# Last two attentions: one group of float32 products for each pair of heads

## The chip, the cores and the metric

The kernel runs on one core of one Trainium2 chip. The metric is the device time of an execution in microseconds; of the kernel before, three runs gave a median of 1101.09 us (1098.07 to 1101.76). One further execution was profiled; all rows of the trace below are from it.

## The reference

Three stages follow one another: attention over four batch entries (called blocks here) with twelve heads, an MLP with squared ReLU, and a router with eight experts of limited capacity. Cut to what is computed:

```python
# q, k, v: [4, 12, 448, 64]
scores = scale * np.matmul(q, k.transpose(0, 1, 3, 2))
scores = cap * np.tanh(scores / cap)
attn = np.exp(scores - np.max(scores, axis=-1, keepdims=True))
attn = attn / (np.sum(attn, axis=-1, keepdims=True) + 1e-09)
x = np.matmul(attn, v)                  # as rows: [1792, 768]
h = x @ w_in                            # 768 -> 2048
r = np.maximum(h, 0.0)
x = (r * r) @ w_out                     # 2048 -> 768
logits = x @ w_gate                     # 768 -> 8
# greedy: the largest logits first, one expert for each token, 224 tokens for each expert
out[mask_e] = np.maximum(x[mask_e] @ w1[e], 0.0) @ w2[e]   # 768 -> 1024 -> 768
```

## The kernel before, in words

**Streams.** `run` works block by block. attention(0) runs alone, hidden(0) beside attention(1), then, for b = 2 and 3, output(b-2) and hidden(b-1) beside attention(b). `merge` interleaves such generators: each yields an amount of TensorE time, and the one that is least far on relative to its total goes next (118.0 for output and hidden together, 44.0 for an attention). For b = 2 and 3 this fixes TensorE's order as written (`manual_schedule` for PE); on the other engines a scheduler orders the instructions. Each engine works through its own queue in order.

**Attention.** A block has six pairs of heads (`hp`). `scores(hp, c)` makes the scores of the pair for a block of keys: for c = 0 to 2 two float32 products with 64 rows, one for each head (L233), for c = 3 one product with 128 rows for the last 64 keys of both heads (L235). They go to a PSUM tile `big`, of which there are two buffers. ScalarE reads it with tanh (L237), which frees the buffer, and makes the exponential in place (L238); sums `z` over the keys are made by VectorE in block 0 and by GpSimd (POOL) in the other blocks (L244, L246, L250). `pv` multiplies with v, in 64 columns for each head (L258) and in full for the last keys (L261), into a PSUM tile `aux`. `norm` sums z over the partitions with two products with ones (L266), also into `aux`; ScalarE adds eps and frees that tile (L268), VectorE takes the reciprocal (L269) and multiplies (L271). `aux` has two buffers as well. `whole = b > 1` marks the blocks 2 and 3; there a pair's float32 products stand on TensorE in three groups, with products of the MLP between: scores 0 and 1 of pair hp; pv and norm of pair hp-1; scores 2 and 3 of pair hp.

**MLP.** Its products, the main products in what follows, are float32r, in three parts (high by high, low by high, high by low): L395 to L397 in `hidden`, 18 for each of 16 weight tiles, and L452 to L454 in `output`, 12 for each of 24 tiles of w_out. `finish` (L430) transposes a finished piece of 128 columns into `aux`, ScalarE copies it (L432) and stores it. Weights arrive as 64-bit integers; for the first block VectorE decodes each tile in three operations (L328 to L330; two buffers `raw`, three `wf`), and stores it to a DRAM cache, from which the later blocks load it. Each tile is split: ScalarE casts the high part `wh` (L356), VectorE or POOL subtracts the low part `wl` (L357), three buffers each. So in the first part of block 2, where output(0) runs beside attention(2), the tiles of w_out are decoded while the attention's tanh and exp share ScalarE's queue with the casts. `split_rows` casts the attention's result into x high and low (L316 for the low part).

Of the kernel before, what the change touches and what calls it, by code (L numbers as in the profile page):

```python
# [23 lines left out]
HP = NH // 2  # L24
# [55 lines left out]
class Kernel:  # L80
# [125 lines left out]
    def attention(self, b):  # L206

        nc, ap = self.nc, self.ap
        qk, P, vt, zs, U = {}, {}, {}, {}, {}
        adder = nc.vector if b == 0 else nc.gpsimd  # L210

        def load(hp):
            qk[hp] = t = ap.tile([128, QK], F32, name="qk", bufs=3)
            if b + hp == 0:
                for half, q in ((0, nc.sync), (1, nc.scalar)):
                    q.dma_start(t[half * 64:half * 64 + 64], self.q_k[b, hp, half * 64:half * 64 + 64])
            else:
                nc.sync.dma_start(t, self.q_k[b, hp])

        def load_v(hp):  # L220
            vt[hp] = ap.tile([128, KB + 1, 2 * DH], F32, name="v", bufs=3)
            nc.sync.dma_start(vt[hp], self.v[b, hp])

        def scores(hp, c):

            t = qk[hp]
            n = 2 if c < KB else 1
            k, q = t[:, c * 128:(c + 1) * 128], t[:, QK - S:]
            ps = self.psum.tile([128, 2, 512], F32, name="big")
            if c < KB:  # L230
                for s in range(2):
                    rows = slice(s * 64, s * 64 + 64)
                    nc.tensor.matmul(ps[:, s, :S], k[rows], q[rows], start=True, stop=True)  # L233
            else:
                nc.tensor.matmul(ps[:, 0, :S], k, q, start=True, stop=True)  # L235
            p = ap.tile([128, n, S], F32, name=f"p{n}", bufs=(2, 5)[n - 1])
            nc.scalar.activation(p, ps[:, :n, :S], AF.Tanh, scale=self.isc)  # L237
            e = nc.scalar.activation(p, p, AF.Exp, scale=self.capt)  # L238
            if b == 0:
                self.exps.append(e)  # L240
            P[hp, c] = p
            if c == 1:
                zs[hp] = z = ap.tile([128, 2, S], F32, name="z", bufs=2)
                adder.tensor_add(z, P[hp, 0], p)  # L244
            elif c == 2:
                adder.tensor_add(zs[hp], zs[hp], p)  # L246
            elif c == KB:
                for s in range(2):
                    half = slice(s * 64, s * 64 + 64)
                    adder.tensor_add(zs[hp][half, s], zs[hp][half, s], p[half, 0])  # L250

        def pv(hp, c0, c1):
            if c0 == 0:
                U[hp] = self.psum.tile([128, S], F32, name="aux")
            for c in range(c0, c1):
                if c < KB:
                    for s in range(2):
                        nc.tensor.matmul(U[hp][s * 64:s * 64 + 64], vt[hp][:, c, s * 64:s * 64 + 64], P[hp, c][:, s],  # L258
                                         start=(c == 0), stop=False, skip_group_check=True)
                else:  # L260
                    nc.tensor.matmul(U[hp], vt[hp][:, c], P[hp, c][:, 0], start=False, stop=True, skip_group_check=True)  # L261

        def norm(hp):
            z = self.psum.tile([128, S], F32, name="aux")
            for s in range(2):
                nc.tensor.matmul(z[s * 64:s * 64 + 64], self.ones, zs[hp][:, s], start=True, stop=True)  # L266
            d = ap.tile([128, S], F32, name="d", bufs=1)
            (nc.vector.tensor_scalar(d, z, self.eps, None, op0=OP.add) if b == 0 else nc.scalar.activation(d, z, AF.Identity, bias=self.eps))  # L268
            nc.vector.reciprocal(d, d)  # L269
            x = self.xq.tile([128, S], F32, name="x")  # L270
            m = nc.vector.tensor_mul(x, U.pop(hp), d)  # L271
            if b == 0:
                self.norms.append(m)
            if b == NB - 1:
                self.mark = m
            self.x_t[b, hp] = x

        load(0)
        load(1)
        load_v(0)  # L280
        whole = b > 1
        for hp in range(HP + 1):
            if hp < HP:
                if hp + 2 < HP:
                    load(hp + 2)
                if hp + 1 < HP:
                    load_v(hp + 1)
                scores(hp, 0)
                if not whole:
                    yield 0.8  # L290
                scores(hp, 1)
                yield 1.6 if whole else 0.8
            if hp:
                pv(hp - 1, 0, 2)
                if not whole:
                    yield 1.6
                pv(hp - 1, 2, 4)
                if not whole or hp == HP:
                    yield 1.6
                norm(hp - 1)  # L300
                yield 4.0 if whole else 0.8
            if hp < HP:
                scores(hp, 2)
                if not whole:
                    yield 0.8
                scores(hp, 3)
                yield 1.4 if whole else 0.6

    def split_rows(self, b):
        nc = self.nc  # L310
# [641 lines left out]
```

## Time and profile before

| what | value |
|---|---|
| median of three runs | 1101.09 us (1098.07 to 1101.76) |
| the profiled execution, its own time | 1098.67 us |
| its span, first to last instruction | 1096.8 us |
| mean granted clock of TensorE | 0.990 |
| busy: TensorE (PE) | 97% |
| busy: VectorE (DVE) | 62% |
| busy: ScalarE (ACT) | 50% |
| busy: GpSimd (POOL) | 32% |

The profiled execution lies 2.4 us under the median. Shares are of the span. Matmuls are pipelined and their ends are modelled, so how long one takes is read from start to start. In the trace's rows an operation names the tile that it writes, an arrow and the tiles that it reads, then the shapes; in square brackets stands how long its engine was idle before it and what ended that. The blocks whose order changes, 2 and 3, run from 187 to 343 and from 359 to 515 us.

### The profile page before, as it was taken

Reading aid. Unit: us, or ns where it says so; the run is one execution under the profiler, and the core shown is the slowest. Engines: PE = TensorE matmul, PEld = TensorE weight load, DVE = VectorE, ACT = ScalarE, POOL = GpSimd, SP = SyncE. Lnnn points to the kernel's source line nnn. Section 1 sums busy time; section 2 is a strip of 40 time slices with the busy share of each in tenths; the row PEclk is TensorE's granted clock in tenths of the full one; section 3 lists DMA queues with packets and bytes.
Section 4 is the critical chain, followed back from the end, with each engine's and each line's share of the span. In section 5 each row is a group of like instructions: output and inputs, shape, how many; then the busy total and the mean of one; then the engine's idle time right before and its main releaser. Section 6 shows DMA issues by size and latency. Waiting matters only on the chain.

```text
span 1096.8 us, 15959 instructions
## 1 busy us (share of the span) xinstructions
PE 1063.3 (97%) x5866; PEld 836.7 (76%) x5866; DVE 676.2 (62%) x1124; ACT 543.8 (50%) x843; POOL 351.0 (32%) x245
## 2 busy tenths in 40 slices
PE   6999999999999999999999999999899999999997
PEld 2336655776677677677787888888799899999996
DVE  5987999978545478788411355565666554555551
ACT  5876776444776744676654222222222223554551
POOL 0127776655221322221443444444210201220000
PEclk9999999999999999999999999999899999999999
DMA  7533655566533377765563233336472465965530
GB/s 278 195 117 124 218 187 203 184 237 232 158 100 95 95 226 245 251 223 200 183 213 95 67 95 103 94 104 213 153 279 70 153 215 179 307 216 185 200 111 26
DMA packets 79454, 187.20 MB, mean 171 GB/s; under 512 B 8528, under 2 KB 19312, under 8 KB 79376
## 3 DMA queue, kind: packets, MB, share of 16 engines
q1 hardware_dynamic: 64736, 169.24, 46.0%
q0 software_dynamic: 3424, 11.19, 3.4%
q10 hardware_dynamic: 11216, 5.75, 2.0%
q8 instruction: 46, 0.75, 0.3%
q14 instruction: 32, 0.26, 0.1%
HBM read 156.26 MB, written 29.88 MB: 170 GB/s over the span
## 4 chain that ended last, share of the span: by engine, by line
PE 65%; issue 12%; DVE 10%; DMA 8%; ACT 2%; POOL 1%; SPq 1%; POOLq 0%; DVEq 0%; ACTq 0%
PE big L877 6%; PE acc L395 6%; PE acc L452 6%; PE acc L396 6%; PE acc L397 6%; PE acc L454 5%; PE acc L453 5%; PE acc L839 5%; PE aux L258 3%; PE big L233 3%; DMA raw<-w_out 3%; PE aux L653 2%; DVE wf L329 2%; DVE wf L328 2%; PE acc L846 2%
## 5 line engine op out<-in xcount | busy, mean ns | idle before, releaser
L356 ACT CAST wh<-wf 128x512 fp32r<-128x512 f32 (+1 forms) x187 | 135.2, 723 | 268.5 <-PE acc L453 102.2
L357 POOL TENSOR_TENSOR wl<-wf,wh 128x512 fp32r<-128x512 f32 (+1 forms) x97 | 156.5, 1616 | 206.5 <-ACT wh L356 196.9
L395 PE MATMUL acc<-xh,wh 128*128 128x448 f32 x384 | 148.6, 389 | 2.0 <-ACT r L402 2.0
L452 PE MATMUL acc<-g,wh 128*128 128x448 f32 x384 | 150.4, 392 | 0.0
L396 PE MATMUL acc<-xl,wh 128*128 128x448 f32 x384 | 141.2, 368 | 1.9 <-DVE xl L316 1.9
L454 PE MATMUL acc<-g,wl 128*128 128x448 f32 x384 | 140.4, 366 | 1.2 <-DVE wl L357 1.2
L397 PE MATMUL acc<-xh,wl 128*128 128x448 f32 x384 | 140.4, 366 | 0.1
L453 PE MATMUL acc<-g,wh 128*128 128x448 f32 x384 | 139.9, 364 | 0.0
L357 DVE TENSOR_TENSOR wl<-wf,wh 128x768 fp32r<-128x768 f32 (+1 forms) x90 | 88.0, 979 | 61.1 <-ACT wh L356 60.3
L877 PE MATMUL big<-wh,g 128*112 128x384 f32 x512 | 117.8, 342 | 0.0
L237 ACT ACTIVATE p<-big,isc 128x896 f32<-128x896 f32 x96 | 85.7, 907 | 26.9 <-PE big L233 26.7
L395 PEld LDWEIGHTS acc<-xh,wh 128*128 128x128 f32 x384 | 72.1, 189 | 35.1 <-issue 15.7
L238 ACT ACTIVATE p<-p,capt 128x896 f32<-128x896 f32 x96 | 89.4, 949 | 1.3
L756 POOL DMA_INDIRECT xg<-x,idx x32 | 34.2, 1068 | 169.9 <-PE acc L775 93.3
L877 PEld LDWEIGHTS big<-wh,g 128*112 128x112 f32 x512 | 86.8, 175 | 0.8
L407 DVE TENSOR_TENSOR g<-r,g 128x448 fp32r<-128x448 f32 x58 | 49.4, 851 | 60.2 <-ACT g L406 57.6
L246 POOL TENSOR_TENSOR z<-z,p 128x896 f32<-128x896 f32 x18 | 38.9, 2162 | 146.4 <-ACT p L238 144.1
L452 PEld LDWEIGHTS acc<-g,wh 128*128 128x128 f32 x384 | 72.4, 189 | 14.4 <-issue 9.6
L396 PEld LDWEIGHTS acc<-xl,wh 128*128 128x128 f32 x384 | 72.6, 189 | 12.4 <-issue 4.1
L269 DVE RECIPROCAL d<-d 128x448 f32<-128x448 f32 x24 | 70.7, 2948 | 16.6 <-ACT d L268 16.5
L233 PE MATMUL big<-qk 64*128 64x448 f32 x288 | 74.1, 598 | 6.9 <-DMA qk<-qk 6.2
L454 PEld LDWEIGHTS acc<-g,wl 128*128 128x128 f32 x384 | 72.0, 187 | 9.4 <-DVE wl L357 2.7
(182 smaller groups left out, 1941.7 us busy)
## 6 DMA issues: line engine op xcount, KB each, us to landing
g<-w SPq DMA_DIRECT2D x68, 384.0 KB
wf<-wi SPq DMA_DIRECT2D x48, 384.0 KB
wf<-wo SPq DMA_DIRECT2D x72, 256.0 KB
wf<-w SPq DMA_DIRECT2D x36, 384.0 KB
raw<-w_in SPq DMA_DIRECT2D x16, 768.0 KB
raw<-w_out SPq DMA_DIRECT2D x24, 512.0 KB
raw<-w_out_t SPq DMA_DIRECT2D x24, 512.0 KB
wt<-wt SPq DMA_DIRECT2D x48, 256.0 KB
```

Source lines behind the costliest of these rows:

```text
L233: nc.tensor.matmul(ps[:, s, :S], k[rows], q[rows], start=True, stop=True)
L237: nc.scalar.activation(p, ps[:, :n, :S], AF.Tanh, scale=self.isc)
L238: e = nc.scalar.activation(p, p, AF.Exp, scale=self.capt)
L356: nc.scalar.copy(wh[:, :w], wf[:, :w])
L357: low.tensor_sub(wl[:, :w], wf[:, :w], wh[:, :w].bitcast(F32))
L395: nc.tensor.matmul(ps, wh[:, d], xh, start=(d == 0), stop=False)
L396: nc.tensor.matmul(ps, wh[:, d], xl, start=False, stop=False)
L397: nc.tensor.matmul(ps, wl[:, d], xh, start=False, stop=(d == ND - 1))
L452: nc.tensor.matmul(ps, a, gh, start=(f == 0), stop=False)
L453: nc.tensor.matmul(ps, a, gl, start=False, stop=False)
L454: nc.tensor.matmul(ps, z, gh, start=False, stop=(f == NF - 1))
L877: nc.tensor.matmul(acc[h][:, s, :DM // 2], l, r[:, s * (DM // 2):(s + 1) * (DM // 2)], start=(j == 0 and first), stop=(j == NF2 - 1 and last))
```

## The change

Only `attention` is edited, and only for `whole`, blocks 2 and 3. From the second pair on, the three groups become one: scores 0 and 1, the first half of pv of the pair before, scores 2, the second half of pv, scores 3, norm, and then a yield of 7.0. The first pair, which has no pair before it, makes its four blocks of scores in a row and yields 3.0. After the last pair pv and norm stand alone as before, with other yields. The amounts add up to about the same for a block, and the interleaving with the MLP changes through them.

```diff
                 scores(hp, 1)
-                yield 1.6 if whole else 0.8
+                if not whole:
+                    yield 0.8
             if hp:
                 pv(hp - 1, 0, 2)
                 if not whole:
                     yield 1.6
+                elif hp < HP:
+                    scores(hp, 2)
                 pv(hp - 1, 2, 4)
                 if not whole or hp == HP:
                     yield 1.6
+                elif hp < HP:
+                    scores(hp, 3)
                 norm(hp - 1)
-                yield 4.0 if whole else 0.8
-            if hp < HP:
+                yield 7.0 if whole else 0.8
+            if hp < HP and not (whole and hp):
                 scores(hp, 2)
                 if not whole:
                     yield 0.8
                 scores(hp, 3)
-                yield 1.4 if whole else 0.6
+                yield 3.0 if whole else 0.6
```

Lines from 306 on are numbered five higher in the changed kernel (L356 becomes L361, L430 becomes L435). On TensorE, at the products with v of pair 2 in block 2 (p_... are the tiles of exponentials, aux the PSUM tile, L452 to L454 main products), the kernel before has a group of its own for them:

```order
L454 MATMUL acc<-g,wl 128x448
L258 MATMUL aux<-p_1724,v 64x448 x2
L258 MATMUL aux<-p_1730,v 64x448 x2
L258 MATMUL aux<-p_1912,v 64x448 x2
L261 MATMUL aux<-p_1918,v 128x448
L266 MATMUL aux<-z,ones 64x448 x2
L452 MATMUL acc<-g,wh 128x448
```

and the changed kernel has:

```order
L459 MATMUL acc<-g,wl 128x448
L233 MATMUL big<-qk 128x448 x4
L258 MATMUL aux<-p_1724,v 64x448 x2
L258 MATMUL aux<-p_1730,v 64x448 x2
L233 MATMUL big<-qk 128x448 x2
L258 MATMUL aux<-p_1743,v 64x448 x2
L261 MATMUL aux<-p_1752,v 128x448
L235 MATMUL big<-qk 128x448
L266 MATMUL aux<-z,ones 64x448 x2
L435 MATMUL aux<-cf,xt 112x128 x4
L457 MATMUL acc<-g,wh 128x448
```

The scores of pair 3 (L233, L235) now stand around the products with v of pair 2, and a `finish` (L435) follows the group.

On ScalarE, the tanh and exp of the same pair 3 (p_1960 is its first block of scores), the kernel before has:

```order
L356 CAST wh<-wf 128x512 x2
L237 ACTIVATE p_1960<-big,isc 128x896
L238 ACTIVATE p_1960<-p_1960,capt 128x896
L237 ACTIVATE p_1966<-big,isc 128x896
L432 COPY rows<-aux 112x512
L238 ACTIVATE p_1966<-p_1966,capt 128x896
```

and the changed kernel:

```order
L361 CAST wh<-wf 128x512 x3
L237 ACTIVATE p_1960<-big,isc 128x896
L238 ACTIVATE p_1960<-p_1960,capt 128x896
L237 ACTIVATE p_1966<-big,isc 128x896
L238 ACTIVATE p_1966<-p_1966,capt 128x896
L237 ACTIVATE p_1979<-big,isc 128x896
L238 ACTIVATE p_1979<-p_1979,capt 128x896
L237 ACTIVATE p_1988<-big,isc 128x448
L238 ACTIVATE p_1988<-p_1988,capt 128x448
L268 ACTIVATE d<-aux,eps 128x448
L437 COPY rows<-aux 112x512
```

Now all eight operations of the pair stand together; ahead of the first tanh stands the cast of w_out tile 20 in both programs.

On VectorE, the reciprocal of pair 1 in block 2 (L269), the kernel before has it among the decodes of w_out tiles (L328 to L330), two tiles later than the changed one:

```order
L357 TENSOR_TENSOR wl<-wf,wh 128x512
L330 SCALAR_TENSOR_TENSOR wf<-raw,wf 128x512
L328 TENSOR_SCALAR wf<-raw 128x512
L329 SCALAR_TENSOR_TENSOR wf<-raw,wf 128x512
L330 SCALAR_TENSOR_TENSOR wf<-raw,wf 128x512
L269 RECIPROCAL d<-d 128x448
L328 TENSOR_SCALAR wf<-raw 128x512
L271 TENSOR_TENSOR x<-aux,d 128x448
```

and the changed kernel:

```order
L335 SCALAR_TENSOR_TENSOR wf<-raw,wf 128x512
L269 RECIPROCAL d<-d 128x448
L362 TENSOR_TENSOR wl<-wf,wh 128x512
L271 TENSOR_TENSOR x<-aux,d 128x448
L333 TENSOR_SCALAR wf<-raw 128x512 x2
L334 SCALAR_TENSOR_TENSOR wf<-raw,wf 128x512 x2
L335 SCALAR_TENSOR_TENSOR wf<-raw,wf 128x512 x2
```

The reciprocal has moved ahead of the decodes of tiles 16 and 17.

## Rows read from the trace of the kernel before

**Rows 1.** The page: busy us, share of the span, instructions of each engine.

```profile
PE 1063.3 (97%) x5866; PEld 836.7 (76%) x5866; DVE 676.2 (62%) x1124; ACT 543.8 (50%) x843; POOL 351.0 (32%) x245
```

**Rows 2.** Windows: length, busy PE, PEld, DVE, ACT, POOL; granted clock, DMA share, GB/s.

```profile
187.00:276.00 89.00, 87.19 (x407) 62.68 (x406) 74.19 (x70) 42.64 (x62) 50.29 (x31) 1.00 0.64 221
```

**Rows 3.** TensorE's waits from 187 to 515: us in total, times, longest.

```profile
PE acc L454 <- DVE wl L357: 1.2, 4, 0.5
PE aux L266 <- ACT rows L432: 1.0, 1, 1.0
```

**Rows 4.** Timeline of TensorE: start, us, instruction (modelled ends); around mode changes.

```profile
25.21 1.72 PE L258 MATMUL aux<-p,v 128*64 128x448 f32 x8
26.86 1.40 PE L233 MATMUL big<-qk 64*128 64x448 f32 x6
...
180.47 0.91 PE L261 MATMUL aux<-p,v 128*128 128x448 f32 x2
180.87 0.71 PE L453 MATMUL acc<-g,wh 128*128 128x448 f32 x1
181.42 0.36 PE L454 MATMUL acc<-g,wl 128*128 128x448 f32 x1
181.62 0.36 PE L452 MATMUL acc<-g,wh 128*128 128x448 f32 x1
...
406.42 1.02 PE L261 MATMUL aux<-p,v 128*128 128x448 f32 x2
407.37 0.97 PE L266 MATMUL aux<-z,ones 128*64 128x448 f32 x4
...
419.58 1.02 PE L235 MATMUL big<-qk 128*128 128x448 f32 x2
420.08 0.72 PE L452 MATMUL acc<-g,wh 128*128 128x448 f32 x1
420.64 0.36 PE L453 MATMUL acc<-g,wh 128*128 128x448 f32 x1
```

**Rows 5.** The same: scores 0 and 1 of two pairs.

```profile
250.71 1.77 PE L233 MATMUL big<-qk 64*128 64x448 f32 x8
...
359.58 1.77 PE L233 MATMUL big<-qk 64*128 64x448 f32 x8
```

**Rows 6.** Timeline of ScalarE: tanh behind these scores.

```profile
256.98 0.62 ACT L356 CAST wh<-wf 128x512 fp32r<-128x512 f32 x1 [4.76 <-DVE wf L330]
257.50 1.00 ACT L237 ACTIVATE p<-big,isc 128x896 f32<-128x896 f32 x1
...
360.74 0.99 ACT L237 ACTIVATE p<-big,isc 128x896 f32<-128x896 f32 x1
...
363.03 1.00 ACT L237 ACTIVATE p<-big,isc 128x896 f32<-128x896 f32 x1
```

**Rows 7.** Timeline of VectorE: decodes of w_out tiles, the last of them tile 20.

```profile
237.50 0.43 DVE L328 TENSOR_SCALAR wf<-raw 128x512 int32<-128x512 int32 x1 [2.61 <-POOL wl L357]
...
252.01 1.60 DVE L328 TENSOR_SCALAR wf<-raw 128x512 int32<-128x512 int32 x1 [0.81 <-DMA raw<-w_out]
253.64 1.67 DVE L329 SCALAR_TENSOR_TENSOR wf<-raw,wf 128x512 int32<-128x512 int32 x1
255.34 1.52 DVE L330 SCALAR_TENSOR_TENSOR wf<-raw,wf 128x512 int32<-128x512 int32 x1
```

**Rows 8.** Windows around an idle stretch of TensorE, columns as in rows 2.

```profile
100.35:102.40 2.05, 0.01 (x1) 0.01 (x1) 2.05 (x2) 0.57 (x2) 0.87 (x1) 1.00 0.00 0
102.57:105.98 3.41, 3.41 (x10) 3.03 (x11) 2.41 (x5) 3.35 (x7) 0.00 (x0) 0.50 0.78 252
```

**Rows 9.** Timeline of ScalarE: the addition of eps that frees a PSUM tile aux.

```profile
381.83 0.64 ACT L268 ACTIVATE d<-aux,eps 128x448 f32<-128x448 f32 x1 [4.72 <-PE aux L266]
```

**Rows 10.** The page's groups: busy us, mean ns of one, idle before and its releaser.

```profile
L269 DVE RECIPROCAL d<-d 128x448 f32<-128x448 f32 x24 | 70.7, 2948 | 16.6 <-ACT d L268 16.5
```

**Rows 11.** Timeline of TensorE: the start of the last hidden layer, behind block 3.

```profile
534.52 0.47 PE L396 MATMUL acc<-xl,wh 128*128 128x448 f32 x1 [1.12 <-DVE xl L316]
```

## What the change does to the time, predicted from the rows

> **What bounds the kernel now.** The page's busy line comes first: TensorE is busy for 97% of the span [rows 1], so a change pays only where it shortens TensorE's own queue or a wait in it. The change touches the attention of blocks 2 and 3 (time 187 to 343 and 359 to 515), and the windows say what stands close behind TensorE there: in block 2's first part, while w_out is still decoded, VectorE is busy for 74.19 of 89 us [rows 2]. The waits that TensorE shows in all of this come to 2.2 us: four times on VectorE's wl (1.2), once on ACT (1.0) [rows 3]. So at most some 2 us of waiting can be won; the rest has to come out of the float32 products themselves.
>
> **Mode changes.** I read starts, since ends are modelled. An L261 (all 128 rows and columns) that stands among the main products, which have the same shape, takes 180.47 to 180.87, and the first main product behind it steps 0.55 instead of 0.20: 0.40 + 0.35 = 0.75 us. Between the 64-column L258 and L266 the same L261 takes 406.42 to 407.37, 0.95; with a change on one side only (L233 ahead of L235, main products behind) it is 0.50 + 0.36 = 0.86 [rows 4]. So a change between 64 rows, 64 columns and the full array costs 0.10 us, and a change of number format alone nothing. Before, a pair has L233 L235 | L233 | L258 L261 L266 with main products between: 2 + 2 + 4 = 8 changes. After it has L233 L258 L233 L258 L261 L235 L266 in one run: 7. That is 0.10 us for each of ten pairs; each block's first pair goes from 4 changes to 2. Sum: -1.0 - 0.4 = **-1.4 us**. L258 directly beside L233 is in the trace (25.21 to 26.86, 1.65 for four products, no extra price [rows 4]). The Trainium skill's TensorEngine Tiling (Key Properties) says that a change of tiling mode drains the array; that speaks against what the change promises, since fewer groups are not fewer modes. If only a group's two ends cost, three groups into one would save 4 changes, 4.4 us in all; the rows bear out the count of modes.
>
> **The first pair's four score blocks in a row.** Scores have two PSUM buffers, so the third block waits for the first block's tanh and the fourth for the second's. In block 3 the first L233 stands at 359.58 and takes 1.7; the third block would start at 361.3, and tanh ends at 361.73: 0.5. The fourth would follow at 362.6; the second tanh (after a cast and an exp) ends at 364.03: 1.4 [rows 5, 6]. 1.9 us in block 3. In block 2 nothing shows it; between 0 and 1.9 I take 0.5, since ACT has no Relu and Square of the hidden layer pending there. Sum **+2.4**.
>
> **The later pairs: is tanh in time?** In the new group the third score block stands behind two score blocks (1.7 [rows 5]) and four products with v (1.65 [rows 4]), so 3.35 us after the group's start; it needs the first tanh done. When ACT is free this holds: the first block is done at 0.95, tanh takes 1.0. The fourth block comes 2.8 us later still and is safe. But ACT works in its queue's order, and ahead of the tanh of pair 3 in block 2 stands the cast of w_out tile 20, in both programs. In the trace that cast stood idle for 4.76 us until VectorE's decode (L330) ended, started at 256.98, and tanh at 257.50, although the scores, started at 250.71, were there from 251.7 [rows 5, 6]. Before, that cost nothing: TensorE came back to this PSUM buffer only 66 main products and all products with v later. After, it is 3.35 us away.
>
> When does the new group of pair 3 start? By the order it stands behind w_out tile 17, and by then TensorE has done exactly what it had done at 250.71 before: the scores of pairs 0 to 2 and v of pairs 0 and 1. So it starts at 250.71 - 0.4 (mode changes) + 0.5 (first pair), less up to 0.8 of the old waits: about 250.2. The third block is due at 253.6. Decode of tile 20 ended at 256.86 before [rows 7]. It may end earlier: its three operations took 1.60, 1.67 and 1.52 beside POOL's sums, while the first takes 0.43 where POOL is idle, so 1.0 us and more can go from each [rows 7], and the sums of that pair now come after its exps; 3.0 us earlier, 253.9, is the early end. It may end later: the reciprocal of pair 1 (2.95 us, as in every pair [rows 10]) now stands ahead of the decode of tiles 16 and 17, and each raw load waits for the decode two tiles before (tile 20's stood idle for 0.81 on its DMA [rows 7]): 259.8 is the late end. Cast 0.5, tanh 1.0 and 0.1 for the semaphores follow: the third block starts at 255.5 to 261.4, a wait of 1.9 to 7.8. I take the decode where the trace has it, a little earlier for the idle POOL: **+5.0 us**. Nothing else is lost behind it, since the weights catch up meanwhile.
>
> **Clock.** After an idle stretch of 2.05 us the trace has the granted clock at 0.50 (1.2 GHz) from 102.57 to 105.98, with ten main products at 0.37 instead of 0.20 [rows 8]: 1.6 us lost. A wait of 5 us should do the same: **+1.5**, between 0 and 1.6. The Trainium skill's TensorE: Matmul & The Clock Gate (Part 1) has the idle array throttled by default and released by activity; by that rule too a wait need not end in a drop each time, and without it the sum is 1.5 lower.
>
> **A transpose right behind the group.** In both blocks L430 now follows the last L266 at once (after pair 3's group). Its PSUM bank is the one that L268 frees; before, six or more main products lay between. L268 starts after L266 and takes 0.64 [rows 9]: at least 0.75 us each. ACT's eight operations of a group (about 1.0 each, half for the last two) end at 8.0 us when on time, as late as the group's products (7.8); behind the late group it is up to 1.7. Sum **+2.2** (1.5 to 3.4).
>
> **The old waits.** The four on wl came where ACT had tanh and exp ahead of a cast while TensorE used up weights; in one group TensorE uses none meanwhile, and after a long wait all tiles are ready. The one on ACT's copy (L266, 1.0) goes since the last transpose now lies at least six products and the group's own 7 us ahead. **-2.2**, with some 0.1 us for each restart -2.5; at least 0.
>
> **Other queues.** SP's loads of qk and v stand behind events that come no later than before (a pair's qk is free at its group's end): 0. POOL's sums of a pair now come in one row, ahead of its wl of tile 6 or 13; TensorE needs tile 6 only 30 main products (6.1 us) behind the group: 0. VectorE's wl of tile 14 stands behind pair 1's reciprocal: 0 to 1.5, kept for the range. After 515 the order is the same in both programs, and TensorE is the bound, so what is gained or lost is carried to the end.
>
> **Sum.** -1.4 + 2.4 + 5.0 + 1.5 + 2.2 - 2.5 = +7.2 us on the profiled execution's 1098.67 (span 1096.8 and 1.9 around it): 1105.9. The median of the runs shown, 1101.09, is 2.4 above that execution, the lowest 0.6 below; I state 1106, on the level of that execution.
>
> **Rivals.** (A) Tile 20 is decoded in time, or pair 3's group comes late enough (point: decode before 252): no wait, no drop. For it: VectorE has 15 us free in 89. Against it: ACT waited there in the trace. -1.4 + 2.4 + 1.5 - 2.5 = 0: 1099, on the median's level 1101; no change. (B) Faster: besides (A), ACT and VectorE drain during the 8 us groups, so that tanh starts within 0.1 us of the scores in the first pairs too (their waits gone) and VectorE's xl behind block 3, which TensorE waits 1.12 us for [rows 11], is in time: -1.4 - 2.5 - 1.1 + 1.5 = -3.5: 1095.2. Against it: Relu, Square and casts stand ahead of tanh in ACT's queue in block 3's first pair too. (C) Slower still: the queue of casts holds tanh in pair 2 as well (the last cast ahead of it is tile 12's, due about when the group starts) or in block 3, where the same queue waits for weights by DMA: another 3 to 5 us, 1110. (D) The change does not do what it says, a group is not cheaper: that is the mode count, and it is in the sum.
>
> **How the numbers follow.** Forecast (pair 3 waits, 1103 to 1109): 0.52. (A) 0.28. (C) 0.12. (B) 0.08. A measurement of this kernel tells about 0.3% (3.3 us) from no change, so faster 0.08, same 0.28, slower 0.64. The range for 8 in 10 takes in the forecast, most of (A) and the lower part of (C): 1098 to 1112.
>
> **What would show it.** In the changed profile: one wait of several us on TensorE between L258 and the third L233 of pair 3 in block 2, ended by ACT's tanh (L237), whose own wait was on VectorE's decode; a granted clock of 0.5 right behind; waits of 0.5 and 1.4 in block 3's first pair; L430 waiting for L268 twice; wl no longer a releaser; the end of each block shifted by +6 and then +1. If pair 3 shows no wait, the forecast is wrong and (A) holds; if TensorE's groups take over 8.3 us without waits, the price of modes is wrong.

## The result, and the profile after

The changed kernel takes 1113.71 us (median of 7 runs, 1106.73 to 1115.52) against 1101.76 us (median of 7): the ratio is 1.0101, with a 95% interval from 1.0077 to 1.0125. It is slower, as forecast, but by 12 us instead of some 5 to 7, and 1.7 us above the range.

The page's busy line (as [rows 1]; us, share of the span, instructions), and TensorE's waits from 187 to 545 us of the changed kernel (as [rows 3]; lines from 306 on are numbered five higher, L435 is the transpose):

```profile
PE 1069.1 (96%) x5866; PEld 843.8 (76%) x5866; DVE 657.6 (59%) x1124; ACT 548.2 (49%) x843; POOL 347.9 (31%) x245
```

```profile
PE big L233 <- ACT p L237: 8.3, 3, 5.4
PE aux L435 <- ACT d L268: 2.1, 2, 1.0
PE big L235 <- ACT p L237: 1.6, 2, 1.3
```

The waits for wl and for ScalarE's copy [rows 3] are gone; 12.0 us of new ones are there. The longest is the one that was forecast. These are the groups of pairs 2 and 3 of block 2 and the first pair of block 3, in TensorE's timeline:

```profile
222.37 1.77 PE L233 MATMUL big<-qk 64*128 64x448 f32 x8
224.08 1.72 PE L258 MATMUL aux<-p,v 128*64 128x448 f32 x8
228.33 1.02 PE L233 MATMUL big<-qk 64*128 64x448 f32 x4 [2.53 <-ACT p L237]
...
253.28 1.77 PE L233 MATMUL big<-qk 64*128 64x448 f32 x8
254.98 1.73 PE L258 MATMUL aux<-p,v 128*64 128x448 f32 x8
262.09 1.86 PE L233 MATMUL big<-qk 64*128 64x448 f32 x4 [5.38 <-ACT p L237]
...
370.25 1.02 PE L233 MATMUL big<-qk 64*128 64x448 f32 x4 [0.43 <-ACT p L237]
372.54 1.38 PE L235 MATMUL big<-qk 128*128 128x448 f32 x2 [1.27 <-ACT p L237]
```

On ScalarE the cast of tile 20 (L361) waits for the decode, and tanh stands behind it, as in [rows 6]; on VectorE that decode waits for its load in turn:

```profile
260.51 0.62 ACT L361 CAST wh<-wf 128x512 fp32r<-128x512 f32 x1 [2.73 <-DVE wf L335]
261.03 1.00 ACT L237 ACTIVATE p<-big,isc 128x896 f32<-128x896 f32 x1
```

```profile
257.57 0.43 DVE L333 TENSOR_SCALAR wf<-raw 128x512 int32<-128x512 int32 x1 [0.53 <-DMA raw<-w_out]
258.04 1.63 DVE L334 SCALAR_TENSOR_TENSOR wf<-raw,wf 128x512 int32<-128x512 int32 x1
259.70 0.69 DVE L335 SCALAR_TENSOR_TENSOR wf<-raw,wf 128x512 int32<-128x512 int32 x1
```

In or right behind each of these three waits the granted clock falls to 0.50. Windows, columns as in [rows 2]; the first answers to that row, the last lies far behind the change, in the experts:

```profile
187.00:276.00 89.00, 79.71 (x353) 54.85 (x353) 74.71 (x68) 44.43 (x62) 51.61 (x32) 0.94 0.60 203
229.70:233.12 3.42, 3.42 (x8) 1.18 (x4) 2.38 (x3) 3.36 (x4) 1.73 (x1) 0.50 0.70 243
260.42:267.25 6.83, 5.16 (x11) 1.66 (x12) 4.79 (x6) 6.44 (x7) 2.08 (x1) 0.50 0.70 232
373.06:376.47 3.41, 3.41 (x10) 2.69 (x9) 0.00 (x0) 3.36 (x6) 2.03 (x1) 0.50 0.39 144
874.82:885.06 10.24, 10.24 (x56) 8.90 (x55) 3.97 (x12) 0.00 (x0) 0.31 (x1) 0.50 0.06 19
```

Half of TensorE's busy time at 0.50 is lost: 1.7 and 2.6 us in block 2, 1.7 in block 3. By the starts of the same products in both traces, the changed kernel is 8.5 us behind at the end of block 2 (its first product of the next block starts at 366.7 instead of 358.3), 10.6 at the start of the last hidden layer, and 10.9 at the last product with w_out (777.6 instead of 766.7). The profiled execution (1115.52) loses another 5.9 in the experts, mostly in the stretch at 874.82. Twelve of the 16 profiled executions of this document have such a stretch, of 6.8 or 10.2 us, that starts between 858 and 875; the kernel before with a third buffer has it, the profiled execution of the kernel before does not. So it is no mark of the change. The medians lie 12.0 apart, near the 10.9 of the last product with w_out; below, the place of the last product with w_out (its shift against the kernel before) stands beside the medians.

### The profile page after: what moved, and what is told of

Same layout as the page of the kernel before. It is cut to its first block, busy times and chain, and to the rows that moved or that the text cites. A ratio compares the mean times of both kernels' runs of the same rounds, so it can differ in the third digit from the quotient of the medians.

```text
span 1113.6 us, 15956 instructions
## 1 busy us (share of the span) xinstructions
PE 1069.1 (96%) x5866; PEld 843.8 (76%) x5866; DVE 657.6 (59%) x1124; ACT 548.2 (49%) x843; POOL 347.9 (31%) x245
## 3 DMA queue, kind: packets, MB, share of 16 engines
q10 hardware_dynamic: 11216, 5.75, 1.9%
## 4 chain that ended last, share of the span: by engine, by line
PE 69%; issue 12%; DVE 7%; DMA 5%; ACT 4%; POOL 2%; SPq 0%; POOLq 0%; ACTq 0%; DVEq 0%
PE acc L400 7%; PE acc L457 6%; PE big L882 6%; PE acc L401 6%; PE acc L402 6%; PE acc L459 6%; PE acc L458 6%; PE acc L844 5%; PE aux L258 4%; PE big L233 4%; PE aux L658 2%; PE aux L261 2%; DVE wf L334 2%; PE acc L851 2%; PE aux L266 1%
## 5 line engine op out<-in xcount | busy, mean ns | idle before, releaser
L361 ACT CAST wh<-wf 128x512 fp32r<-128x512 f32 (+1 forms) x187 | 135.4, 724 | 308.2 <-PE acc L458 121.6
L400 PE MATMUL acc<-xh,wh 128*128 128x448 f32 x384 | 146.0, 382 | 2.0 <-ACT r L407 2.0
L362 DVE TENSOR_TENSOR wl<-wf,wh 128x768 fp32r<-128x768 f32 (+1 forms) x90 | 80.4, 896 | 68.5 <-ACT wh L361 67.5
L882 PE MATMUL big<-wh,g 128*112 128x384 f32 x512 | 120.3, 348 | 0.0
L244 POOL TENSOR_TENSOR z<-p,p 128x896 f32<-128x896 f32 x18 | 39.1, 2174 | 202.3 <-issue 152.6
L269 DVE RECIPROCAL d<-d 128x448 f32<-128x448 f32 x24 | 70.8, 2949 | 40.8 <-ACT d L268 40.7
L233 PE MATMUL big<-qk 64*128 64x448 f32 x288 | 75.1, 606 | 15.3 <-ACT p L237 9.1
L402 PEld LDWEIGHTS acc<-xh,wl 128*128 128x128 f32 x384 | 72.5, 189 | 6.4 <-issue 0.8
```

The source lines that it names most:

```text
L361: nc.scalar.copy(wh[:, :w], wf[:, :w])
L362: low.tensor_sub(wl[:, :w], wf[:, :w], wh[:, :w].bitcast(F32))
L400: nc.tensor.matmul(ps, wh[:, d], xh, start=(d == 0), stop=False)
L402: nc.tensor.matmul(ps, wl[:, d], xh, start=False, stop=(d == ND - 1))
L882: nc.tensor.matmul(acc[h][:, s, :DM // 2], l, r[:, s * (DM // 2):(s + 1) * (DM // 2)], start=(j == 0 and first), stop=(j == NF2 - 1 and last))
```

## The experiments

Ratios are against the kernel before, with their 95% intervals; shifts are of the last product with w_out, in the traces. When block 2 starts, ahead of every edit to the attention, the traces already lie between 1.0 us ahead of that of the kernel before and 0.3 us behind it, so a difference of less than 1 us between two shifts says nothing.

**Block 3 alone, block 2 alone.** The new grouping for one block only (`one = b == 3`, then `one = b == 2`, against the changed kernel):

```diff
-                if not whole:
-                    yield 0.8
+                if not one:
+                    yield 1.6 if whole else 0.8
...
-                elif hp < HP:
+                elif one and hp < HP:
...
-                yield 7.0 if whole else 0.8
-            if hp < HP and not (whole and hp):
+                yield (7.0 if one else 4.0) if whole else 0.8
+            if hp < HP and not (one and hp):
...
-                yield 3.0 if whole else 0.6
+                yield (3.0 if one else 1.4) if whole else 0.6
```

> Only block 3 has the one group per pair; block 2 keeps the three groups of before. Theory (TensorE waits for tanh, and tanh waits behind casts of w_out that wait for decode): no decode in block 3, so only the first pair's waits (0.4 and 1.3 us), one transpose wait (1.0) and a clock drop (1.7), less what the fewer changes of tiling save: about +2 us at the end of block 3, median 1102 to 1104. Rival (the long float32 run itself is what costs, about evenly in both blocks): +5 us, 1106 to 1108.

> Only block 2 has the one group per pair. Theory: the waits of 2.5 and 5.4 us for tanh in pairs 2 and 3 and their clock drops are all here: +8.5 us at the end of block 2 as in the changed kernel, median 1108 to 1112. Rival (cost is even over both blocks): +5 us, 1106 to 1108.

Block 3 alone: 1101.82, ratio 0.9987 (0.9965 to 1.0008), shift +1.4. Block 2 alone: 1111.52, ratio 1.0075 (1.0047 to 1.0103), shift +8.3. The cost is block 2's, where w_out is decoded; in block 3 the long groups cost nothing that a measurement can tell.

**Casts off ScalarE.** Five casts that stand ahead of the late tanh go to VectorE:

```diff
-        nc.scalar.copy(wh[:, :w], wf[:, :w])
+        early = self.ready - self.at[0, "o"] in (11, 12, 18, 19, 20)
+        (nc.vector.tensor_copy if early else nc.scalar.copy)(wh[:, :w], wf[:, :w])
```

> The changed kernel, with five casts of w_out (tiles 11, 12, 18, 19, 20) made by VectorE right behind the decode instead of by ScalarE, so that no cast that is late stands ahead of the tanh of pairs 2 and 3 in block 2. Theory: the waits of 2.5 and 5.4 us and the two drops behind them (1.7 and 2.4) go, block 2 ends 3 us or more earlier than in the kernel before rather than 8.5 later, median 1101 to 1104. Rival (decode itself is too slow for the bunched demand, and the wait only moves): TensorE then waits as long for wh or wl of tiles 13 or 21, and the median stays at 1110 or above.

1110.21, ratio 1.0088 (1.0061 to 1.0115), shift +9.6. Here the theory that I had fell. Its waits:

```profile
PE acc L460 <- DVE wl L363: 2.6, 1, 2.6
PE acc L458 <- ACT wh L362: 2.2, 1, 2.2
PE aux L436 <- ACT d L268: 2.1, 2, 1.0
PE big L235 <- ACT p L237: 1.6, 2, 1.3
PE acc L460 <- POOL wl L363: 1.2, 3, 0.6
...
PE big L233 <- ACT p L237: 0.6, 2, 0.4
```

Of the 7.9 us for tanh in pairs 2 and 3 nothing is left, and 6.0 us for wl and wh have come up on the main products. The order on ScalarE decided which instruction waits, not that one has to. What is short is decoded w_out: the new theory, supply. The run is not a clean test of it, since the five casts are 3.9 us of new work for VectorE, the engine that decodes; the shorter decode and the third buffer, below, leave the casts where they were.

**The first pair in two groups, as before.**

```diff
                 scores(hp, 1)
                 if not whole:
                     yield 0.8
+                elif hp == 0:
+                    yield 1.6
...
-                yield 3.0 if whole else 0.6
+                yield 1.4 if whole else 0.6
```

> The changed kernel, but the first pair of blocks 2 and 3 makes its scores in two groups, as before. Theory: the first pair's waits for a PSUM buffer (0.3 in block 2; 0.4 and 1.3 in block 3) and the drop behind the last (1.7) go, four changes of tiling come back: 2.5 to 3.5 us less than the changed kernel, median 1110 to 1112; pairs 2 and 3 of block 2 wait as before. Rival (the wait of 1.3 comes from casts that ScalarE makes late in block 3, not from the buffers): the wait moves to the second group and the time stays.

1109.86, ratio 1.0065 (1.0042 to 1.0088), shift +5.2 against +10.9. From the start of block 2 to the last hidden layer it gives back 4.1 us: its own waits and drop (2.0 and 1.7), and in pair 2 the drop and some of the wait, which falls from 2.53 to 1.77; on the other side stand 1.5 us of new waits for a wl on POOL and four changes of tiling. The supply shows why pair 2 gains: in the changed kernel POOL's sums of the first pair come earlier, and a wl, which frees a buffer wf, starts at 191.27 behind the first of them instead of at 189.01 ahead of it:

```profile
189.18 2.12 POOL L244 TENSOR_TENSOR z<-p,p 128x896 f32<-128x896 f32 x1 [2.39 <-ACT p L238]
191.27 1.29 POOL L362 TENSOR_TENSOR wl<-wf,wh 128x512 fp32r<-128x512 f32 x1
```

and in the kernel before:

```profile
189.01 1.29 POOL L357 TENSOR_TENSOR wl<-wf,wh 128x512 fp32r<-128x512 f32 x1 [2.18 <-ACT wh L356]
190.26 2.09 POOL L244 TENSOR_TENSOR z<-p,p 128x896 f32<-128x896 f32 x1
```

The decode of tile 6 that needs the buffer ends at 199.7 instead of 195.1 (194.3 in this run). So a lag is there before pair 1 ends, 26 us ahead of pair 2's wait. But it is not all of it: in this run tile 6 is on time, and tile 9 is late all the same (214.0 instead of 209.6), since POOL's sums of pair 1 stand in one row too, from 202.03 on, and the wl behind them starts only at 209.51:

```profile
207.08 2.35 POOL L250 TENSOR_TENSOR z<-z,p 64x448 f32<-64x448 f32 x2
209.51 2.53 POOL L364 TENSOR_TENSOR wl<-wf,wh 128x512 fp32r<-128x512 f32 x2
```

The first of these two ends at 210.79, and the next decode of w_out starts on VectorE at 210.82, after 2.22 us of idle time. So pairs 2 and 3 still wait, 1.77 and 5.75 us.

**A shorter decode.** The third decode operation is left out for w_out:

```diff
-        nc.vector.scalar_tensor_tensor(o, lo, 29, o, op0=OP.logical_shift_right, op1=OP.bitwise_or)
+        if self.loaded not in range(self.at[0, "o"], self.at[0, "o"] + ND * OB):
+            nc.vector.scalar_tensor_tensor(o, lo, 29, o, op0=OP.logical_shift_right, op1=OP.bitwise_or)
```

> The changed kernel with one part of the work left out: the third of the three decode operations of the 24 tiles of w_out (L335, 0.69 to 2.5 us each), so these weights lack their three lowest bits. The casts stay ahead of tanh on ScalarE. Theory S (supply: the decode hands over tiles with a few us to spare at best, stands still at full buffers while a group of 8 us uses no weights, and the shortage shows at whatever waits first): with 0.7 us or more saved for each tile the waits of 7.9 us in pairs 2 and 3 shrink to 3 or less, median 1104 to 1108. Theory Q (the order of ScalarE's queue alone, as I had it): the cast still stands ahead of tanh and comes about 1 us earlier for each of the two pairs, waits of 6 remain, median 1110 to 1112.

**A third buffer raw.**

```diff
-tc.tile_pool(name="rows", bufs=ND + 1, side="right")
+tc.tile_pool(name="rows", bufs=ND, side="right")
...
-name="raw", bufs=2
+name="raw", bufs=3
```

> The changed kernel with a third buffer raw for the encoded weights (and one buffer less for rows, to make room). It tells which part of the supply is short. If it is the load, which starts only when a raw buffer is free (VectorE stood idle for 0.5 to 1.5 us on it ahead of most decodes): the waits in pairs 2 and 3 of block 2 fall to 4 us or less, median 1106 to 1110. If it is VectorE's own time, or the buffers behind the decode: waits of 7 to 8 us and 1112 to 1114 as in the changed kernel.

Shorter decode: 1103.73, ratio 1.0010 (0.9989 to 1.0031), shift -1.3. Third buffer: 1103.52, ratio 1.0029 (1.0006 to 1.0053), shift +1.8. Both take away 9 to 12 us of shift, and the wait of pair 3 falls to 1.0 us in both, with the casts still ahead of tanh. With two buffers a load starts when the decode two tiles before has ended (in the changed kernel that of tile 16 at 246.3, the load behind it at 246.8), so a shorter decode brings the loads forward as well, and the two runs do not tell which half is the slower one. VectorE's waits in block 2's first part (187 to 275), in the changed kernel and then with the third buffer:

```profile
DVE wf L333 <- DMA raw<-w_out: 7.3, 7, 1.5
DVE wf L333 <- issue: 4.4, 1, 4.4
```

```profile
DVE wl L362 <- ACT wh L361: 6.4, 1, 6.4
DVE wf L333 <- DMA raw<-w_out: 3.2, 4, 1.7
```

The 4.4 us have no releaser in the trace; they end at 251.4, 4.6 us after that load was issued, so most likely they are a load too. In the kernel before VectorE waits 8.2 us for loads, so such waits alone do not tell the two kernels apart.

The same as a table, end of the decode and start of TensorE's products for some tiles, in us of each trace:

| tile of w_out | before | changed | changed, third buffer |
|---|---|---|---|
| 6 | 195.1, 209.0 | 199.7, 210.7 | 199.1, 210.1 |
| 10 | 211.4, 221.7 | 218.3, 221.0 | 218.0, 220.3 |
| 16 | 239.9, 243.9 | 246.3, 248.3 | 241.8, 245.1 |
| 20 | 256.9, 263.3 | 260.4, 275.4 | 252.9, 268.2 |
| 23 | 268.9, 271.2 | 273.9, 283.2 | 264.0, 275.9 |

Before, a tile is decoded 2 to 14 us ahead of its use. Changed, tile 10 has 2.7 left instead of 10.3 (the third buffer does not mend that, 2.3; it brings the tiles behind it forward), and tile 12 (decoded at 225.7) is still to come when pair 2 starts at 222.4, and tiles 19 and 20 (257.0 and 260.4) when pair 3 starts at 253.3. Tile 20 is used 15 us after its decode: the main product was never the late one, the tanh behind its cast was.

**The two on the kernel before,** as a control.

> The kernel before with a third buffer raw (one buffer rows less), nothing else. Theory S: with three groups for each pair TensorE takes the tiles more evenly, and the waits that a better supply can take away in block 2 are 1.8 us; so -2 to -4 us, and the gain of 10 us that the same buffer gave the changed kernel is for the most part the change's own loss. Rival (a general gain, with nothing to do with the grouping): -8 to -10 us here too.

> The kernel before with the third decode operation of the 24 tiles of w_out left out, as in the run on the changed kernel, so that these weights lack their three lowest bits. Theory S: -2 us, the old waits of block 2. Rival (general gain): -8 to -10 us.

Third buffer: 1097.40, ratio 0.9967 (0.9947 to 0.9987), shift -4.0. Shorter decode: 1099.59, ratio 0.9985 (0.9966 to 1.0003), shift -4.5. That is the far end of what was expected of the one (-2 to -4) and more than was expected of the other (-2), because the old waits cost more than the time that TensorE stood idle in them. One of those for wl:

```profile
402.47 0.36 PE L453 MATMUL acc<-g,wh 128*128 128x448 f32 x1
403.01 0.47 PE L454 MATMUL acc<-g,wl 128*128 128x448 f32 x1 [0.17 <-DVE wl L357]
403.31 0.36 PE L452 MATMUL acc<-g,wh 128*128 128x448 f32 x1
```

The product that waited starts 0.54 us behind the one ahead of it and the next 0.30 behind that, both 0.20 without a wait: 0.44 us for 0.17 of idle time. Counted so, the old waits between 187 and the last hidden layer cost 3.7 us, and over the same stretch the third buffer gives the kernel before 4.0. So the kernel before was short of w_out too; but of the 9.1 and 12.2 us that the two runs gave the changed kernel, 5.1 and 7.7 are the change's own.

**Both causes taken from the changed kernel:** a third buffer raw, and the first pair in two groups.

> The changed kernel with its two causes of waits taken away: a third buffer raw for the supply of w_out, and the first pair in two groups. By theory S the waits of 7.9 us in block 2 are 2 or less and those of the first pair (2.0 with a drop in block 3) are gone, so that what is left are the transposes behind the groups (about 3 us): median 1100 to 1102, level with the kernel before. Should the long group itself cost, it stays at 1104 or more.

1101.32, ratio 0.9980 (0.9958 to 1.0001), shift -1.3: level with the kernel before, as expected, and above the kernel before with the same buffer (-4.0). What is left are the transposes behind the groups (3.3 us), 1.0 for tanh and 0.7 for wl on POOL.

**What a change of tiling costs.** On the kernel before, in blocks 2 and 3 only, the ones ahead of the full product with v (first `norm`, below); then the full product ahead of the others (`pv`):

```diff
+            if whole:
+                pv(hp, KB, KC)
...
-                pv(hp - 1, 2, 4)
+                pv(hp - 1, 2, KB if whole else KC)
```

> The kernel before with one thing moved, and no other grouping: in blocks 2 and 3 the products with ones (64 columns) stand ahead of the last product with v (full), so that a pair has six changes of tiling instead of eight. 24 changes fewer. At 0.10 us for a change, as the prediction had it: -2.4 us. At 0.18, as the changed kernel's groups have it when what stands on both sides of a change is counted: -4.3 us, median 1097 to 1099 against 1101.8. Rival (it is the number of groups that counts, not of changes): no change at the end of block 3.

```diff
-            for c in range(c0, c1):
+            order = range(c0, c1) if not whole else [(KB, 0), (1, 2)][c0 // 2]
+            first, last = (0, KB) if not whole else (KB, KB - 1)
+            for c in order:
...
```

> The kernel before with one thing moved in blocks 2 and 3: the full product with v (L261) stands first among a pair's products with v, not between the 64-column ones. Nothing else moves on any other engine, and the ones stay where they were, so that the wait of 2.8 us for a PSUM tile, which cost the run with the ones moved its gain in block 2, should stay at 1.0. Two changes of tiling fewer for each of 12 pairs. At 0.18 us each: -4.3 us at the end of block 3, median 1096 to 1098 against 1101.3. At 0.10: -2.4, 1098.5 to 1099.5.

The ones first: 1099.97, ratio 0.9984 (0.9965 to 1.0004), shift -1.1; the ones now wait 2.8 us for a tile aux instead of 1.0, and a clock drop of 3.4 us follows. In its block 3 it saves 2.7 us, of which 0.9 are two old waits for wl that it lacks. The full product first: 1100.24, ratio 0.9977 (0.9963 to 0.9990), shift -1.9. In its block 3 the waits are those of before, and ten changes fewer save 1.7 us, 0.17 each. There are ten and not 12 because the last pair's norm stands alone: its two groups have four changes in any of these orders, and they take as long as before. A whole group of it, from the last main product ahead to the second behind, takes 403.43 to 407.94, 4.51 us:

```profile
403.43 0.37 PE L456 MATMUL acc<-g,wl 128*128 128x448 f32 x1
403.63 0.91 PE L263 MATMUL aux<-p,v 128*128 128x448 f32 x2
404.48 2.48 PE L260 MATMUL aux<-p,v 128*64 128x448 f32 x12
406.78 0.92 PE L268 MATMUL aux<-z,ones 128*64 128x448 f32 x4
407.63 0.47 PE L454 MATMUL acc<-g,wh 128*128 128x448 f32 x1
407.94 0.37 PE L455 MATMUL acc<-g,wh 128*128 128x448 f32 x1
```

The group of [rows 4] at 406.42 takes 403.72 to 408.58 in the kernel before, 4.86:

```profile
403.72 0.36 PE L454 MATMUL acc<-g,wl 128*128 128x448 f32 x1
404.01 2.48 PE L258 MATMUL aux<-p,v 128*64 128x448 f32 x12
...
408.27 0.47 PE L452 MATMUL acc<-g,wh 128*128 128x448 f32 x1
408.58 0.36 PE L453 MATMUL acc<-g,wh 128*128 128x448 f32 x1
```

0.35 us for two changes, 0.17 each again; the same group with the ones first takes 4.52. In block 2 the gain went into waits: 4.2 us from 187 to 515 instead of 2.2 [rows 3], the longest 1.6 for a wl.

**Fewer changes in longer groups.** In block 3 one group with four changes, block 2 with the ones first (`norm`, with `one = b == 3`):

```diff
+            if one and hp + 1 < HP:
+                scores(hp + 1, 2)
+            if whole:
+                pv(hp, KB, KC)
+            if one and hp + 1 < HP:
+                scores(hp + 1, 3)
...
-                yield 1.6 if whole else 0.8
+                if not (one and hp):
+                    yield 1.6 if whole else 0.8
...
-                pv(hp - 1, 2, 4)
+                pv(hp - 1, 2, KB if whole else KC)
...
-                yield 4.0 if whole else 0.8
-            if hp < HP:
+                yield (7.0 if one else 4.0) if whole else 0.8
+            if hp < HP and not (one and hp):
```

> Block 3 alone has one group per pair from the second pair on, in an order with four changes of tiling (scores 0 and 1, then all 64-column products with the ones last, then scores 2, the full products); its first pair has two groups as before. Block 2 keeps three groups, with the ones ahead of the last product with v. At 0.18 us for a change: block 2 saves 2.2, block 3 about 3.6 and loses nothing to the first pair; one transpose behind a group waits up to 1 us. Sum -5 us: median 1096 to 1098 against 1101.8, faster than both kernels. Rival (at 0.10 for a change, and a tanh that is late in block 3's groups too): -1 us or none.

A miss: 1110.12, ratio 1.0066 (1.0044 to 1.0088), shift +9.0. Block 3 now waits for wl on VectorE, 3.56 us at the worst, since the scheduler put that wl behind the reciprocal and a decode of wt, tiles that another stream prepares for the gates:

```profile
504.44 0.47 PE L405 MATMUL acc<-xh,wl 128*128 128x448 f32 x1 [3.56 <-DVE wl L365]
```

```profile
496.78 2.94 DVE L275 RECIPROCAL d<-d 128x448 f32<-128x448 f32 x1
...
502.23 1.29 DVE L338 SCALAR_TENSOR_TENSOR wt<-raw,wt 128x512 int32<-128x512 int32 x2
503.44 0.95 DVE L365 TENSOR_TENSOR wl<-wf,wh 128x768 fp32r<-128x768 f32 x1
```

The price of a change comes out here as well: the one group, with four changes, takes 7.93 us where no wait falls into it (from 371.75), that of the changed kernel, with seven, 8.41 (from 382.07): 0.16 each.

**Three groups or two, with a third buffer raw.** First the kernel with the full product first and the third buffer; then the same, with scores 2 and 3 right behind `norm`:

```diff
                 norm(hp - 1)
-                yield 4.0 if whole else 0.8
-            if hp < HP:
+                if whole and hp < HP:
+                    scores(hp, 2)
+                    scores(hp, 3)
+                yield 5.4 if whole else 0.8
+            if hp < HP and not (whole and hp):
```

> The same with a third buffer raw (one buffer rows less). If the load of w_out holds the decode up in the kernel before as well, its waits for wl and for ScalarE's copy in block 2 (0.3, 0.5 and 1.0 us) go too: 1 to 2 us less than with two buffers. If TensorE is the only bound there, the same time as with two.

> The same again with three buffers raw, and from the second pair on two groups for each pair: scores 0 and 1; then the full product with v, the 64-column ones, the ones, scores 2 and 3, in 5.4 us. Five changes of tiling for each pair instead of six: -1.8 us against the three groups at 0.18 each, if the longer hole (5.4 us instead of 3.9) costs no wait; if the supply of w_out is short at it, a wait of 2 us or more in block 2 eats that, and the time is that of the three groups or above.

Three groups: 1094.64, ratio 0.9919 (0.9902 to 0.9935), shift -8.0: faster than both kernels, by 7 to 9 us and by 19 us. In TensorE's waits from 187 to 515 one is left of [rows 3]:

```profile
PE acc L456 <- DVE wl L359: 0.7, 1, 0.7
```

Two groups: 1100.22, ratio 0.9967 (0.9945 to 0.9988), shift -5.0. Over block 2 alone they gain 1.2 us on the three groups (their trace was 0.7 us behind at its start and is 0.5 ahead at its end), of which five changes fewer explain 0.9; in block 3 three waits of 1.4 for wl on VectorE eat it. A longer hole needs slack in every stream that runs beside it.

## Why the prediction was wrong, step by step

Against the start of the last hidden layer (10.6 us late; waits and half-clock stretches as quoted, the old waits at what they cost from start to start; the first row is what remains):

| term | predicted | measured |
|---|---|---|
| changes of tiling, fewer groups | -1.4 | -3.7 |
| first pairs: waits | +2.4 | +2.0 |
| first pair of block 3: clock drop | none | +1.7 |
| pair 2 of block 2: wait and drop | a rival, (C) | +2.5 and +1.7 |
| pair 3 of block 2: wait and drop | +5.0 and +1.5 | +5.4 and +2.6 |
| transposes behind groups | +2.2 | +2.1 |
| old waits | -2.5 | -3.7 |
| sum | +7.2 | +10.6 |

**Right:** the bound, the direction, the place of the wait in pair 3, the waits of the first pair in block 3 (0.43 and 1.27 for 0.5 and 1.4), both transposes, and that wl would go from the list of releasers. That nothing is lost behind pair 3's wait held too: no later wait of block 2 is for weights, and tiles 18 to 23 are ready 9 to 17 us ahead. The size of pair 3's wait (5.4 for 5.0) is in part luck: the group started 3.1 us later than forecast (253.3 for 250.2), the decode of tile 20 ended 3.5 later than taken (260.4 for 256.9) and behind the stated late end of 259.8, and only the difference came out right.

**The step that failed** is the term under "Other queues" that puts POOL's sums in one row at 0, and with it the decodes of all tiles but tile 20, which I left where the trace of before has them. I asked when TensorE needs tile 6, and not what the wl behind those sums sets free. The runs showed that it frees a buffer for the next decode: the wl comes 2.3 us later and the decode of tile 6 ends 4.6 us later; each load waits for one of two buffers raw; and TensorE, which takes no weights for 8 us, then takes a tile in 2.4 where decodes end 4.3 us apart (tile 6 to 20, 60.7 us for 14). So tile 12, "due about when the group starts", was decoded at 225.7 and not at 219.7, its cast held pair 2's tanh, and that cost a wait of 2.5 us and a drop of 1.7. The prediction has this case only as rival (C), with 0.12. It is the same shortage as pair 3's and should have stood in the same sum: with it (4.2 us) the forecast would have been 1110. The 74 of 89 us of [rows 2] were the sign, read only as room. That the supply is the cause, and not ScalarE's order or the long group, is shown by the runs that speed it up; how the lag of each tile divides between POOL's sums, the loads and the decode is not settled.

**The clock** was mis-sized: one drop in the sum, three in the trace. The one in block 3 follows waits of 0.43 and 1.27 us, shorter than the 2.05 of [rows 8], and it did not have to come: four other traces (block 3 alone, the casts, the shorter decode, the third buffer) have the same two waits at the same place, and the clock stays at 1.00. In the same way waits of 1.0 and 2.2 us in pair 3's group are followed by a drop with the third buffer and by none with the shorter decode. So the 1.7 us of this row belong to the profiled execution and not to the change; what decides it stays open. That the Trainium skill (TensorE: Matmul & The Clock Gate, Part 1) has activity release the throttle agrees: in each of the three stretches at 0.50, of 3.4 to 6.8 us, TensorE is at work again, and behind it the clock is at 1.00.

**The changes of tiling and the old waits** gave back more than forecast, by 2.3 and 1.2 us, which hid part of the miss. Of a change I read what the product ahead of it loses, 0.10 us; the first product behind it loses too, and three runs give 0.16 to 0.17 each. The rule of the Trainium skill (TensorEngine Tiling, Key Properties) that a change of mode drains TensorE agrees: two of these runs kept the 19 groups of a block, and had only fewer changes of mode. 14 changes make 2.4 of the 3.7 us. Groups cost a little besides: a pair's three groups took 2.31, 4.87 and 2.31 us before, from the last main product ahead to the second behind, less 0.81 for the four main products that two more groups bring into this count 8.68; the one group takes 8.41. That is 0.27 less for each of ten pairs, 0.17 for its one change and 0.10 for two groups fewer, and 1.0 us in all for the latter. Some 0.3 us are left over. For each restart after a wait I had 0.1 us; the trace has nearly 0.3 between main products.

**The rest:** 12 instead of 10.9 at the median, and 17 in the profiled execution, arise in the experts behind the change; of the 5.9 us there in the profiled execution 5.1 are the half-clock stretch that other kernels show too. The remaining 1 us at the median is small against the spread of the runs (1106.73 to 1115.52).

## What to carry to other kernels

Before work is bunched on the engine that bounds, compare the pace of whatever feeds it: with tiles ready 2 us ahead at the narrowest place, a hole of 8 us is paid back at the next instruction that stands behind the feeder, whichever that is. Moving that instruction moves the wait; a third buffer for the loads took most of it away, and gave 4 us to the kernel that nobody had changed. Count changes of tiling, and order products within the groups that exist before making groups longer.

## What was not expected of the hardware

- A product of 128 rows and columns placed next to main products of that shape instead of between 64-column ones saves 0.35 us for each pair whose norm stands in the same group: 1.7 us in the ten changes of block 3.
- A wait of 1.27 us, 1.0 us behind one of 0.43, was followed by 3.4 us at a granted clock of 0.50, which cost as much (1.7 us) as both waits; four other traces with the same two waits show no drop.
- A wait of 0.17 us between two main products cost 0.44 from start to start.
- One decode operation of 128x512 elements (L333 of the changed kernel) took 0.43 us at 257.57, where POOL was idle until 257.85, and 2.35 at 204.22, the latter while POOL was in a sum of 128x896 (L246, 203.83 to 206.29).
